# Attention steps at other units, two banks for the output sums alone, and the norm weights transposed first

## The chip, the cores and the metric

The kernel runs on one core of a Trainium2 chip. The metric is the device time of one execution in microseconds. Before the change it is 291.34 us, the median of three runs (291.09 to 291.55). The profile is of one further execution, with a span of 290.2 us from its first to its last instruction; times "at 48.06" are microseconds from the start of that span.

## The reference

Linear attention with a normalisation, and then a two-layer feed-forward network with a PReLU in between:

```python
# q, k, v: (8 batches, 8 heads, 576 positions, 64), g_norm: (64,)
kv  = np.einsum('bhsd,bhse->bhde', k, v)
o   = np.einsum('bhsd,bhde->bhse', q, kv)
rms = np.sqrt(np.mean(o * o, axis=-1, keepdims=True) + 1e-06)
x   = (o / rms * g_norm)          # to (4608 tokens, 512)
h   = x @ w_in                    # (4608, 2048)
g   = np.maximum(h, 0.0) + alpha * np.minimum(h, 0.0)
out = g @ w_out                   # (4608, 512), float32
```

## The kernel before

The 4608 tokens are handled in 9 windows of 512 (`W = 512`, w = 0 to 8). Heads go in pairs (j = 0 to 3), two heads of 64 filling the 128 rows. Window 0 is worked off by itself. From window 1 on there is one loop: in each of 16 units (`u`) of window w, TensorE makes one group of 128 hidden features of window w, some of the second product of window w - 1, and a few attention steps of window w + 1.

PSUM, where all matmuls write, is divided into pools of one 128x512 float32 bank each; a tag names one bank, or as many as `bufs` says:

```python
ps_h = ...  # tags h0, h1, h2: hidden groups (later also sums of the second product)
ps_y = ...  # tag y
ps_s = ctx.enter_context(tc.tile_pool(name="pss", bufs=1, space=bass.MemoryType.PSUM))
ps_o = ctx.enter_context(tc.tile_pool(name="pso", bufs=2, space=bass.MemoryType.PSUM))
ps_q = ctx.enter_context(tc.tile_pool(name="psq", bufs=1, space=bass.MemoryType.PSUM))
...
Q_POOL, S_POOL, O_POOL = (ps_q, "q"), (ps_s, "s"), (ps_o, "o")
```

The four attention steps of a pair. Each ends with an instruction on another engine that reads the bank; until that is done, no later tile can have the bank. `ot_ps` is held longest: by its square, and by the norm, which comes after the sum of squares.

```python
def step_t(b, j, pool=(ps_s, "s")):          # q transposed
    qt_ps = pool[0].tile([P, n_runs(b) * rows(b)], FP16, name="qt_ps", tag=pool[1])
    ...                                       # 5 transposes (6 in batch 0)
    nc.scalar.copy(out=qts[b, j][:], in_=qt_ps[:, 0:S])   # VectorE for b == 0 and j < 2

def step_kv(b, j, pool=(ps_s, "s")):
    kv_ps = pool[0].tile([P, P], FP32, name="kv_ps", tag=pool[1])
    ...                                       # 5 matmuls (6 in batch 0)
    nc.vector.tensor_mul(out=kvs[b, j][:], in0=kv_ps[:], in1=mask32[:])

def step_ot(w, j, pool=None):                 # output sums, without a pool: ps_o
    ot_ps = ps_o.tile([P, W], FP32, name="ot_ps", tag="o")
    ...                                       # one matmul for each batch in the window
    nc.scalar.activation(out=sq[:], in_=ot_ps[:], func=AF.Square)

def ssq_mm(w, j, pool=(ps_s, "s")):           # sum of squares, 1/sqrt
    nc.tensor.matmul(out=ssq_ps[:], lhsT=mask16[:], rhs=sq[:], start=True, stop=True)
    nc.scalar.activation(out=rstd[:], in_=ssq_ps[:], func=AF.Abs_reciprocal_sqrt, ...)

def norm(w, j):                               # frees ot_ps
    nc.vector.scalar_tensor_tensor(out=xts[w, j][:], in0=ot_ps[:], scalar=g2col[:],
                                   in1=rstd[:], op0=ALU.mult, op1=ALU.mult)
# step_ssq(w, j, pool) is ssq_mm and then norm
```

A hidden group (`h_ps`, `m_sb`, `gt` in the profile): four matmuls, a Relu on ScalarE into one of two `m_sb` buffers, and a VectorE instruction that frees the bank:

```python
def m1_group(w, g, pool=None):
    ...                                                   # 4 matmuls into h_ps
    nc.scalar.activation(out=m_sb[:], in_=h_ps[:], func=AF.Relu, scale=-1.0)
    nc.vector.scalar_tensor_tensor(out=gts[w, i][:, r, :], in0=m_sb[:],
        scalar=beta_sb[:, g : g + 1], in1=h_ps[:], op0=ALU.mult, op1=ALU.add)
```

The loop, cut to what concerns window 1 (all engines run their instructions in program order):

```python
Y3_AT = [(8, 8), (8, 8), (8, 8), (8, 9), (9, 9), (9, 10), (10, 10), (10, 10), (10, 11),
         (11, 11), (11, 12), (12, 12), (12, 13), (13, 14), (14, 15), (15, 16)]
for w in range(1, NW):
    ...
    for u in range(NF):                      # 16 units
        m1_group(w, G_ORDER[u])
        ...
        if w == 1 and u == 2:
            regroup(2, "k", 0, H)
        if w == 1 and u == NF - 1:
            regroup(3, "q", 0, 2)
        if w == 2 and u == 0:
            h_tags[0] = ("h1", "h2")         # from here two banks for hidden groups
        if w == 1:
            for i in range(*Y3_AT[u]):       # the last quarter of window 0's product
                y_mm(ys[3], 0, 3, i)
                if i == NF - 1:
                    y_out(ys[3], 0, 3)       # ScalarE copies the bank out
        else:
            ...                              # 7 matmuls of window w - 1
        attention(w + 1, u)
        if w == 1:
            for k in {5: (0,), 8: (1,)}.get(u, ()):
                s_sum(1, 1, k)               # two VectorE instructions on
                s_sum(1, 2, k)               #   what units 0 to 7 made
        ...
```

The front, before window 0's hidden groups (`keep_warm` is matmuls whose result nobody reads; `alpha_row` holds alpha and g_norm, loaded by three small transfers at the very start):

```python
    step_t(0, 0, h_at(0))
    keep_warm(2)
    step_kv(0, 0)
    keep_warm(1)
    step_ot(0, 0)
    regroup0("q", 1)
    keep_warm(1)
    step_t(0, 1, h_at(1))
    regroup0("k", 1)
    ssq_mm(0, 0)
    keep_warm(1)
    step_kv(0, 1, h_at(2))
    keep_warm(1)
    step_ot(0, 1)
    ...                        # alpha_ps, see the change
    step_t(0, 2, h_at(0))
    step_t(0, 3, h_at(1))
    ...                        # g2col, beta_sb and norm(0, 0), see the change
    ssq_mm(0, 1, h_at(2))
    keep_warm(2)
    regroup0("k", 2, 2)
    step_kv(0, 2, h_at(0))
    keep_warm(1)
    step_kv(0, 3, h_at(1))
    norm(0, 1)
    step_ot(0, 2, (ps_y, "y"))
    ...
```

After that come the hidden groups of window 0, and then three quarters of its second product, mixed with the attention steps of window 1, which need batch 1 of q, k and v.

Of the kernel before, what the change touches and what calls it, by code (L numbers as in the profile page):

```python
# [9 lines left out]
FP32 = mybir.dt.float32  # L10
FP16 = mybir.dt.float16
AF = mybir.ActivationFunctionType
ALU = mybir.AluOpType
# [4 lines left out]
def kernel(  # L18
# [11 lines left out]
    nc = tc.nc  # L30
# [5 lines left out]
    P = 128  # L36
# [10 lines left out]
    NF = D_FF // P  # L47
# [4 lines left out]
    const_p = ctx.enter_context(tc.tile_pool(name="constp", bufs=1))  # L52
# [10 lines left out]
    ps_y = ctx.enter_context(tc.tile_pool(name="psy", bufs=1, space=bass.MemoryType.PSUM))  # L63
# [11 lines left out]
    def early_pair(eng, nm, tag):  # L75
# [14 lines left out]
            name=nc.get_next_instruction_name(),  # L90
# [18 lines left out]
    alpha_row = ysb_p.tile([P, D_MODEL], FP32, name="y_sb")  # L109
    nc.sync.dma_start(out=alpha_row[0:NF, 0:P], in_=moe_alpha[:].rearrange("(g p) -> g p", p=P))  # L110
    for r in range(P // D):
        nc.sync.dma_start(
            out=alpha_row[NF : NF + 1, r * D : (r + 1) * D], in_=g_norm[:].unsqueeze(0)
# [7 lines left out]
    for i in range(NBUF):  # L121
        t = {}
# [39 lines left out]
    def load_batch(b, names=("k", "v", "q")):  # L162
        for nm in names:
            load_rem(b, nm)
            load_main(b, nm)

    def regroup0(nm, j, n=1):
        i, h = divmod(2 * j, HH)
        nc.vector.tensor_copy(  # L169
            out=bufs[0][nm][0:P0, :, 2 * j : 2 * (j + n), :].rearrange("p t h d -> p h t d"),  # L170
            in_=stages[0, nm, i][0:P0, h : h + 2 * n],
        )
# [40 lines left out]
    ident = const_p.tile([P, P], FP32, name="ident")  # L213
# [19 lines left out]
    def keep_warm(n, ps=warm_ps):  # L233
        for i in range(n):
            nc.tensor.matmul(out=ps[:], lhsT=warm16[:, 0:P], rhs=warm16, start=True, stop=True)
# [8 lines left out]
    def rows(b):  # L244
        return P0 if b == 0 else P

    def n_runs(b):
        return T0 if b == 0 else NT

    def pair_cols(b, nm, j):  # L250
        def f(t):
            n = rows(b)
            if nm == "v" and b == 0:
                h = 2 * j % HH
                return stages[b, nm, 2 * j // HH][0:n, h : h + 2, t, :]
            if nm == "v" and t < TPP:
                return stages[b, nm][:, 2 * j : 2 * j + 2, t, :]
            if nm == "v":
                return bufs[b % NBUF][nm][0:n, 0, 2 * j : 2 * j + 2, :]
            return bufs[b % NBUF][nm][0:n, t, 2 * j : 2 * j + 2, :]  # L260
        return f

    def step_t(b, j, pool=(ps_s, "s")):
        qs = pair_cols(b, "q", j)
        qt_ps = pool[0].tile([P, n_runs(b) * rows(b)], FP16, name="qt_ps", tag=pool[1])
        c = 0
        for t in range(n_runs(b)):
            n = rows(b)
            nc.tensor.matmul(  # L269
                out=qt_ps[:, c : c + n],  # L270
                lhsT=qs(t),
                rhs=ident16[0:n, 0:n],
                is_transpose=True,
                start=(t == 0),
                stop=(t == n_runs(b) - 1),
            )
            c += n
        qts[b, j] = attn_p.tile([P, S], FP16, name="qt_sb", tag=f"qt{j}")
        if b == 0 and j < 2:
            nc.vector.tensor_copy(out=qts[b, j][:], in_=qt_ps[:, 0:S])  # L280
        else:
            nc.scalar.copy(out=qts[b, j][:], in_=qt_ps[:, 0:S])  # L282

    def step_kv(b, j, pool=(ps_s, "s")):
        ks, vs = pair_cols(b, "k", j), pair_cols(b, "v", j)
        kv_ps = pool[0].tile([P, P], FP32, name="kv_ps", tag=pool[1])
        for t in range(n_runs(b)):
            nc.tensor.matmul(  # L288
                out=kv_ps[:],
                lhsT=ks(t),  # L290
                rhs=vs(t),
                start=(t == 0),
                stop=(t == n_runs(b) - 1),
            )
        kvs[b, j] = attn_p.tile([P, P], FP16, name="kv_sb", tag=f"kv{j}")
        nc.vector.tensor_mul(out=kvs[b, j][:], in0=kv_ps[:], in1=mask32[:])
# [26 lines left out]
    def ssq_mm(w, j, pool=(ps_s, "s")):  # L323
        ot_ps, sq = ots.pop((w, j))
        ssq_ps = pool[0].tile([P, W], FP32, name="ssq_ps", tag=pool[1])
        nc.tensor.matmul(out=ssq_ps[:], lhsT=mask16[:], rhs=sq[:], start=True, stop=True)  # L326
        rstd = attn_p.tile([P, W], FP32, name="rstd")
        nc.scalar.activation(  # L328
            out=rstd[:], in_=ssq_ps[:], func=AF.Abs_reciprocal_sqrt, bias=eps_t[:], scale=inv_d,
        )  # L330
        ots[w, j] = (ot_ps, rstd)

    def norm(w, j):
        ot_ps, rstd = ots.pop((w, j))
        xts[w, j] = xt_p.tile([P, W], FP16, name="xt", tag=f"xt{j}")
        nc.vector.scalar_tensor_tensor(  # L336
            out=xts[w, j][:], in0=ot_ps[:], scalar=g2col[:], in1=rstd[:],
            op0=ALU.mult, op1=ALU.mult,
        )
# [210 lines left out]
    Q_POOL, S_POOL, O_POOL = (ps_q, "q"), (ps_s, "s"), (ps_o, "o")  # L550

    def cast0(nm, eng_copy):
        eng_copy(
            out=bufs[0][nm][0:P0, :, 0:2, :].rearrange("p t h d -> p h t d"),
            in_=st32[nm][0:P0].rearrange("p h (t d) -> p h t d", t=T0),
        )

    def h_at(i):
        return (ps_h, f"h{i}")

    cast0("q", nc.vector.tensor_copy)
    cast0("k", nc.scalar.copy)
    step_t(0, 0, h_at(0))
    keep_warm(2)
    step_kv(0, 0)
    keep_warm(1)
# [7 lines left out]
    step_kv(0, 1, h_at(2))  # L574
    keep_warm(1)
    step_ot(0, 1)
    alpha_ps = ps_y.tile([P, NF + 1], FP32, name="alpha_ps", tag="y")
    nc.tensor.matmul(
        out=alpha_ps[:], lhsT=alpha_row[0 : NF + 1, 0:P], rhs=ident[0 : NF + 1, 0 : NF + 1],
        is_transpose=True, start=True, stop=True,  # L580
    )
    regroup0("q", 2, 2)
    keep_warm(1)
    step_t(0, 2, h_at(0))
    step_t(0, 3, h_at(1))
    g2col = const_p.tile([P, 1], FP32, name="g2col")
    nc.vector.tensor_copy(out=g2col[:], in_=alpha_ps[:, NF : NF + 1])
    beta_sb = const_p.tile([P, NF], FP32, name="beta_sb")
    nc.vector.tensor_scalar(
        out=beta_sb[:], in0=alpha_ps[:, 0:NF], scalar1=-1.0, scalar2=1.0, op0=ALU.mult, op1=ALU.add,  # L590
    )
    norm(0, 0)
    ssq_mm(0, 1, h_at(2))
    keep_warm(2)
    regroup0("k", 2, 2)
# [108 lines left out]
            ATT_AT.setdefault(3 * j + at, []).append((what, j))  # L704
    ATT_1 = {}
    for what, ats in (
        ("t", (0, 2, 4, 5)), ("kv", (4, 5, 6, 7)), ("ot", (6, 8, 10, 12)), ("ssq", (9, 10, 12, 14))
    ):
        for j, at in enumerate(ats):
            ATT_1.setdefault(at, []).append((what, j))  # L710
    ATT = {"t": step_t, "kv": step_kv, "ot": step_ot, "ssq": step_ssq}

    def attention(w, u):
        if w < NW:
            for what, j in (ATT_1 if w == 2 else ATT_AT).get(u, ()):
                if w < B or what in ("ot", "ssq"):
                    if w == 2 and what in ("kv", "ssq"):
                        pool = Q_POOL if j % 2 == 0 else O_POOL if what == "kv" else S_POOL
                        (step_kv if what == "kv" else step_ssq)(w, j, pool)
                    else:  # L720
                        ATT[what](w, j)
# [9 lines left out]
    for w in range(1, NW):  # L731
        if w + 2 < B:
            load_batch(w + 2)
        for u in range(NF):
            m1_group(w, G_ORDER[u])
            if w > 1:
                unit_sums(w, u)
# [5 lines that stand above are left out]
                h_tags[0] = ("h1", "h2")  # L743
            if w > 2 and u == 0:
                y_read(w - 2, "c12")
            if w == 1:
                for i in range(*Y3_AT[u]):
                    y_mm(ys[3], 0, 3, i)
                    if i == NF - 1:
                        y_out(ys[3], 0, 3)  # L750
            else:
                for i in range(u * PER, (u + 1) * PER):
                    prod_mm(w - 1, *Y_LIST[i])
                for what in Y_READS.get(u, ()):
                    y_read(w - 1, what)
            attention(w + 1, u)
            if w == 1:
                for k in {5: (0,), 8: (1,)}.get(u, ()):
                    s_sum(1, 1, k)
                    s_sum(1, 2, k)  # L760
            if w + 2 < B:
                for nm, j in REG_AT.get(u, ()) if w > 1 else ():
                    regroup_pair(w + 2, nm, j)
            if w == 2:
                for nm, j in REG_2.get(u, ()):
                    regroup_pair(3, nm, j)
                if u < 2:
                    s_sum(1, u + 1, 2)
# [48 lines left out]
```

## Time and profile before

| | before |
|---|---|
| time, median of 3 | 291.34 us (291.09 to 291.55) |
| span of the profile | 290.2 us |
| TensorE matmul busy | 280.6 us (97%) |
| VectorE busy | 221.2 us (76%) |
| ScalarE busy | 177.2 us (61%) |
| TensorE clock granted | 0.999 |
| first h matmul of window 0, 1, 2 | 16.14, 48.06, 69.10 us |

In the profile's lines, PE is TensorE (PEld its weight loads), DVE is VectorE, ACT is ScalarE, POOL is GpSimd, and L352 is line 352 of the kernel. A line of a timeline gives the start, the duration, the engine, the source line, what is written from what, and the idle time before it with what ended it. A line of the chain gives start, duration and what it was. Matmuls are pipelined: the duration of a row reaches beyond the start of the next one.

### The profile page before, as it was taken

To read this page: it belongs to the slowest core of one execution; us is meant where nothing else is said; L and a number is where in the kernel's file an instruction comes from. 1 tells how busy PE (TensorE), PEld (TensorE's weight loads), DVE (VectorE), ACT (ScalarE), POOL (GpSimd) and SP (SyncE) were. 2 spreads that over 40 slices of the span, in tenths; PEclk is the share of its full clock that TensorE was granted. 3 is DMA by queue.
4 is the path that set the end of the run, shared out by engine and by line. 5 is a ranking of instruction groups with operands and counts; after the bars stand their busy time and mean duration, and the time that the engine had idled before them with its cause. 6 is when DMAs were issued, how large, how long until landed. Compare 5 with 4: busy or idle time off the path is not lost.

```text
span 290.2 us, 5214 instructions
## 1 busy us (share of the span) xinstructions
PE 280.6 (97%) x1988; PEld 179.5 (62%) x1988; DVE 221.2 (76%) x420; ACT 177.2 (61%) x307; POOL 50.1 (17%) x72
## 2 busy tenths in 40 slices
PE   7899999989999999999999999999999999999994
PEld 2444544634766666667766667666666666666783
DVE  6569729878688878797778777877878788787862
ACT  2567448768878865785678668765754565443310
POOL 8743334760023210212012000000000000000001
PEclk9999999999999999999999999999999999999999
DMA  7999999999709990199019401110112011201223
GB/s 153 194 207 195 198 201 193 179 184 189 111 6 119 189 160 3 39 179 170 3 38 146 118 0 37 38 61 15 37 29 77 5 38 36 63 11 37 67 81 109
DMA packets 50397, 28.43 MB, mean 98 GB/s; under 512 B 13524, under 2 KB 50020, under 8 KB 50372
## 3 DMA queue, kind: packets, MB, share of 16 engines
q0 software_dynamic: 40064, 18.98, 50.4%
q1 hardware_dynamic: 9396, 8.24, 9.7%
q10 hardware_dynamic: 912, 0.89, 1.1%
q8 instruction: 15, 0.25, 0.3%
q14 instruction: 10, 0.08, 0.1%
HBM read 36.71 MB, written 9.44 MB: 159 GB/s over the span
## 4 chain that ended last, share of the span: by engine, by line
PE 83%; DMA 12%; DVE 1%; issue 1%; ACT 1%; POOL 1%; DVEq 0%; POOLq 0%
PE h_ps L352 38%; PE yY L501 14%; PE yZ L501 10%; PE yX L501 9%; DMA vst<-in_v_dram 5%; DMA w_in_sb<-in_moe_w_in_dram 5%; PE kv_ps L288 3%; PE ot_ps L310 3%; DMA qst<-in_q_dram 2%; PE ssq_ps L326 2%; PE qt_ps L269 2%; PE y L377 2%; DVE gt L363 1%; ACT m_sb L359 1%; DVE xt L336 0%
## 5 line engine op out<-in xcount | busy, mean ns | idle before, releaser
L352 PE MATMUL h_ps<-xt,w_in_sb 128*128 128x512 f16 x576 | 145.5, 379 | 0.5 <-DVE gt L363 0.3
L363 DVE SCALAR_TENSOR_TENSOR gt<-m_sb,beta_sb,h_ps 128x512 f16<-128x512 f32 x144 | 106.9, 745 | 45.9 <-ACT m_sb L359 44.3
L359 ACT ACTIVATE m_sb<-h_ps 128x512 f32<-128x512 f32 x144 | 86.0, 598 | 60.3 <-PE h_ps L352 46.8
L352 PEld LDWEIGHTS <-w_in_sb 128*128 128x128 f16 x576 | 54.4, 98 | 45.9 <-issue 1.4
L501 PEld LDWEIGHTS <-s 128*128 128x128 f16 x512 | 50.1, 98 | 19.3
L501 PEld LDWEIGHTS <-gt 128*128 128x128 f16 x384 | 37.6, 98 | 15.1 <-issue 0.5
L501 PE MATMUL yY<-wsum,s 128*128 128x256 f16 x256 | 36.3, 273 | 0.0
L501 PE MATMUL yX<-w_out_sb,gt 128*128 128x256 f16 x256 | 35.1, 273 | 0.0
L316 ACT ACTIVATE sq_sb<-ot_ps 128x512 f16<-128x512 f32 x36 | 21.3, 597 | 17.3 <-PE ot_ps L310 16.8
L328 ACT ACTIVATE rstd<-ssq_ps,eps_t 128x512 f32<-128x512 f32 x36 | 24.6, 688 | 9.7 <-PE ssq_ps L326 9.7
L336 DVE SCALAR_TENSOR_TENSOR xt<-ot_ps,g2col,rstd 128x512 f16<-128x512 f32 x36 | 26.5, 744 | 4.3 <-ACT rstd L328 4.3
L400 POOL DMA_DIRECT2D out_dram<-y_sb x8 | 4.4, 550 | 139.1 <-DVE y_sb L526 131.4
L282 ACT COPY qt_sb<-qt_ps 128x576 f16<-128x576 f16 x30 | 18.7, 637 | 5.8 <-PE qt_ps L269 5.7
L501 PE MATMUL yY<-wsum,gt 128*128 128x256 f16 x128 | 17.6, 273 | 0.0
L501 PE MATMUL yZ<-w_out_sb,s 128*128 128x256 f16 x128 | 17.6, 273 | 0.0
L501 PE MATMUL yZ<-wsum,s 128*128 128x256 f16 x128 | 17.6, 273 | 0.0
L377 PE MATMUL y<-w_out_sb,gt 128*128 128x512 f16 x64 | 17.1, 379 | 0.4 <-DMA w_out_sb<-in_moe_w_out_dram 0.3
L310 PE MATMUL ot_ps<-qt_sb,kv_sb 128*128 128x512 f16 (+7 forms) x64 | 13.7, 286 | 1.5 <-DVE xt L336 0.8
L143 POOL DMA_DIRECT2D vst<-in_v_dram x7 | 6.2, 888 | 48.4 <-PE kv_ps L288 44.8
L288 PEld LDWEIGHTS <-ksb 128*128 128x128 f16 (+1 forms) x164 | 11.4, 98 | 4.5 <-DVE ksb L169 1.5
L288 PE MATMUL kv_ps<-vst,ksb 128*128 128x128 f16 (+1 forms) x136 | 12.6, 219 | 1.4 <-DMA vst<-in_v_dram 0.8
L453 DVE TENSOR_TENSOR s<-s,gt 128x512 f16<-128x512 f16 x32 | 13.5, 421 | 0.5
(67 smaller groups left out, 243.0 us busy)
## 6 DMA issues: line engine op xcount, KB each, us to landing
out_dram<-y_sb SPq DMA_DIRECT2D x72, 64.0 KB, 2.2
kst<-in_k_dram POOLq DMA_DIRECT2D x7, 512.0 KB, 6.8
qst<-in_q_dram POOLq DMA_DIRECT2D x7, 512.0 KB, 10.2
vst<-in_v_dram POOLq DMA_DIRECT2D x7, 512.0 KB, 8.7
out_dram<-y_sb SPq DMA_DIRECT2D x23, 128.0 KB, 2.0
w_out_sb<-in_moe_w_out_dram POOLq DMA_DIRECT2D x4, 512.0 KB, 16.1
w_in_sb<-in_moe_w_in_dram POOLq DMA_DIRECT2D x3, 512.0 KB, 12.1
w_in_sb<-in_moe_w_in_dram POOLq DMA_DIRECT2D x2, 256.0 KB, 8.3
```

What stands on the lines that cost most here:

```text
L282: nc.scalar.copy(out=qts[b, j][:], in_=qt_ps[:, 0:S])
L288: nc.tensor.matmul(out=kv_ps[:], lhsT=ks(t), rhs=vs(t), start=(t == 0), stop=(t == n_runs(b) - 1),)
L310: nc.tensor.matmul(out=ot_ps[:, n0 - w * W : n1 - w * W], lhsT=kvs[b, j][:], rhs=qts[b, j][:, n0 - b * S : n1 - b * S], start=True, stop=True,
L316: nc.scalar.activation(out=sq[:], in_=ot_ps[:], func=AF.Square)
L328: nc.scalar.activation(out=rstd[:], in_=ssq_ps[:], func=AF.Abs_reciprocal_sqrt, bias=eps_t[:], scale=inv_d,)
L336: nc.vector.scalar_tensor_tensor(out=xts[w, j][:], in0=ot_ps[:], scalar=g2col[:], in1=rstd[:], op0=ALU.mult, op1=ALU.mult,)
L352: nc.tensor.matmul(out=h_ps[:], lhsT=w_in_blk(c, g), rhs=xts[w, c][:], start=(c == 0), stop=(c == NC - 1),)
L359: nc.scalar.activation(out=m_sb[:], in_=h_ps[:], func=AF.Relu, scale=-1.0)
L363: nc.vector.scalar_tensor_tensor(out=gts[w, i][:, r, :], in0=m_sb[:], scalar=beta_sb[:, g : g + 1], in1=h_ps[:], op0=ALU.mult, op1=ALU.add,)
L377: nc.tensor.matmul(out=y[:], lhsT=gt_cols(w, g, a * P, (a + 1) * P), rhs=w_out_blk(g), start=(g == 0), stop=(g == NF - 1),)
L453: nc.vector.tensor_sub(out=t[:], in0=sums[w, 1, k][:], in1=a11)
L501: nc.tensor.matmul(out=bank, lhsT=lhs, rhs=rhs, start=fresh, stop=(c == NK - 1), skip_group_check=True,)
```

## The change

It has two parts.

Block 1, the loop over window 1: the attention steps of window 2 move to other units. The kv steps of pairs 1 and 3, which took one of the two `ps_o` banks, take the bank of `ps_s`, so that both `ps_o` banks serve output sums alone. The outputs of pairs 0 and 1 are then made in the same unit, and the first sum of squares follows one unit after it. Two sums on VectorE move from unit 8 to unit 7. It is meant to let the output steps find a free bank.

| step of window 2 | units before, pairs 0 to 3 | units after |
|---|---|---|
| t | 0, 2, 4, 5 | 0, 2, 4, 7 |
| kv | 4, 5, 6, 7 | 4, 5, 6, 8 |
| ot | 6, 8, 10, 12 | 7, 7, 11, 12 |
| ssq and norm | 9, 10, 12, 14 | 8, 10, 12, 13 |

The front: the transpose of alpha and g_norm on TensorE, and the two VectorE instructions that read it (`g2col`, `beta_sb`), come right after the first transpose step. The norm of pair 0 comes directly behind the regroup of q for pairs 2 and 3. It is meant to take two instructions and a wait out of VectorE's way before the regroup of k.

```diff
     step_t(0, 0, h_at(0))
+    alpha_ps = ps_y.tile([P, NF + 1], FP32, name="alpha_ps", tag="y")
+    nc.tensor.matmul(
+        out=alpha_ps[:], lhsT=alpha_row[0 : NF + 1, 0:P], rhs=ident[0 : NF + 1, 0 : NF + 1],
+        is_transpose=True, start=True, stop=True,
+    )
+    g2col = const_p.tile([P, 1], FP32, name="g2col")
+    nc.vector.tensor_copy(out=g2col[:], in_=alpha_ps[:, NF : NF + 1])
+    beta_sb = const_p.tile([P, NF], FP32, name="beta_sb")
+    nc.vector.tensor_scalar(... alpha_ps[:, 0:NF] ...)
     keep_warm(2)
     step_kv(0, 0)
...
     step_ot(0, 1)
-    alpha_ps = ...             # the same matmul
     regroup0("q", 2, 2)
+    norm(0, 0)
     keep_warm(1)
     step_t(0, 2, h_at(0))
     step_t(0, 3, h_at(1))
-    g2col = ...                # the same two instructions
-    beta_sb = ...
-    norm(0, 0)
     ssq_mm(0, 1, h_at(2))
     keep_warm(2)
     regroup0("k", 2, 2)
...
     for what, ats in (
-        ("t", (0, 2, 4, 5)), ("kv", (4, 5, 6, 7)), ("ot", (6, 8, 10, 12)), ("ssq", (9, 10, 12, 14))
+        ("t", (0, 2, 4, 7)), ("kv", (4, 5, 6, 8)), ("ot", (7, 7, 11, 12)), ("ssq", (8, 10, 12, 13))
     ):
...
                     if w == 2 and what in ("kv", "ssq"):
-                        pool = Q_POOL if j % 2 == 0 else O_POOL if what == "kv" else S_POOL
+                        pool = Q_POOL if j % 2 == 0 else S_POOL
...
             if w == 1:
-                for k in {5: (0,), 8: (1,)}.get(u, ()):
+                for k in {5: (0,), 7: (1,)}.get(u, ()):
                     s_sum(1, 1, k)
                     s_sum(1, 2, k)
```

The second part uses `attention(w + 1, u)`, in which the steps of a unit stand in the order t, kv, ot, ssq.

More of the change, by code (lines that the diff above doesn't have):

```diff
@@ L563 @@
     step_t(0, 0, h_at(0))
+    alpha_ps = ps_y.tile([P, NF + 1], FP32, name="alpha_ps", tag="y")
[6 more added lines that the diff above has]
+    beta_sb = const_p.tile([P, NF], FP32, name="beta_sb")
+    nc.vector.tensor_scalar(
+        out=beta_sb[:], in0=alpha_ps[:, 0:NF], scalar1=-1.0, scalar2=1.0, op0=ALU.mult, op1=ALU.add,
+    )
     keep_warm(2)
@@ L576 @@
     step_ot(0, 1)
[L577 to L581, printed above, removed]
     regroup0("q", 2, 2)
+    norm(0, 0)
     keep_warm(1)
@@ L585 @@
     step_t(0, 3, h_at(1))
[L586 to L591, printed above, removed]
-    norm(0, 0)
     ssq_mm(0, 1, h_at(2))
```

## The prediction

> **What bounds the kernel now.** I read the page first, then the chain of waits in order of time, then the timeline of single engines around the two places that the change touches. The page's busy times and its chain of waits:
>
> ```profile
> span 290.2 us, 5214 instructions
> PE 280.6 (97%) x1988; PEld 179.5 (62%) x1988; DVE 221.2 (76%) x420; ACT 177.2 (61%) x307; POOL 50.1 (17%) x72
> PE 83%; DMA 12%; DVE 1%; issue 1%; ACT 1%; POOL 1%; DVEq 0%; POOLq 0%
> ```
>
> TensorE sets the time: 83% of the chain is its own work. What can be won lies in the other 17%. 12% is DMA, and the chain in order of time puts it at the start (rows for 1.32 to 38.80 us). VectorE and ScalarE have 1% each; read off the chain's pieces, some 3.6 us of theirs lie between 57.8 and 62.7 us, in the loop over window 1, whose attention steps for window 2 are what the diff moves (the others are near 42 and 71 us, outside of it). The chain there:
>
> ```profile
> 48.22 0.86 PE h_ps L352 x4
> 49.09 0.28 PE qt_ps L269 x5
> ...
> 52.24 0.22 PE y L377
> ...
> 53.59 0.28 PE kv_ps L288 x5
> ...
> 56.65 0.22 PE ot_ps L310 x2
> ...
> 57.77 0.61 ACT m_sb L359
> 58.38 0.02 issue
> 58.40 0.75 DVE gt L363
> 59.15 0.21 DVE kv_sb L296
> 59.36 0.04 issue
> 59.40 0.38 PE ot_ps L310 x2
> ...
> 61.31 0.75 DVE gt L363
> 62.06 0.67 DVE xt L336
> 62.73 0.05 issue
> 62.78 0.39 PE ot_ps L310 x2
> 63.17 0.21 PE ssq_ps L326
> ```
>
> The first rows give what each step costs TensorE when it flows: 0.86 us for the four matmuls of a unit, 0.28 for a transpose step, 0.28 for a kv step, 0.22 each for an ot step, a sum of squares and a y matmul. The lower rows show the chain leaving TensorE twice, each time to come back at an ot step. TensorE's timeline shows the size of the two holes:
>
> ```profile
> 58.71 0.38 PE L377 MATMUL y<-w_out_sb,gt 128*128 128x512 f16 x1
> 59.40 0.38 PE L310 MATMUL ot_ps<-qt_sb,kv_sb 128*128 128x128 f16 x2 [0.31 <-DVE kv_sb L296]
> ...
> 61.56 0.38 PE L377 MATMUL y<-w_out_sb,gt 128*128 128x512 f16 x1
> 62.78 0.39 PE L310 MATMUL ot_ps<-qt_sb,kv_sb 128*128 128x128 f16 x2 [0.84 <-DVE xt L336]
> ```
>
> A y matmul blocks the array for 0.22, so ot of pair 1 could have started at 58.93 and started at 59.40 (0.47 lost), and ot of pair 2 at 61.78 instead of 62.78 (1.00 lost). As a cross-check, the stage runs from 48.06 (first matmul of window 1) to 69.10 (first of window 2), 21.04 us; its work is 16 x 0.86 + 8 x 0.22 + 4 x (0.28 + 0.28 + 0.22 + 0.22) = 19.52, so 1.52 idle, and the two holes are 1.47 of it.
>
> For the front, the same TensorE timeline further ahead:
>
> ```profile
> 35.74 2.75 PE L377 MATMUL y<-w_out_sb,gt 128*128 128x512 f16 x12 [0.32 <-DMA w_out_sb<-in_moe_w_out_dram]
> 38.85 0.40 PE L288 MATMUL kv_ps<-vst,ksb 128*128 128x128 f16 x4 [0.36 <-DMA vst<-in_v_dram]
> ```
>
> TensorE waits twice for a transfer here: for the second quarter of w_out, then for v of batch 1. In the chain, a queue of loads (1.32 to 10.48 q, 10.76 to 24.45 w_in, 24.99 to 38.80 v) is the whole path up to 38.80.
>
> **What the Trainium skill says.** "TensorE: Matmul & The Clock Gate", Single matmul latency and Back-to-back issue gap: a warm matmul of N columns takes (398 + N)/2.4 ns alone and N/2.4 + 2.5 apart when they follow each other; for 512 that is 379 and 216. The trace agrees with both (mean 379 ns on the h_ps rows, 0.86 / 4 = 0.215 us in the chain); the lower sustained figure that the page also gives, 131 ns, is not seen here. So I count TensorE by steps of 0.216, not by its rows. "Perfetto Trace Analysis", Optimizing Scalar/DVE Operations: the profiled latency is longer than what the engine is held for, because the acknowledgement of the write overlaps the next instruction. The trace agrees: ScalarE rows of 0.60 follow each other 0.49 to 0.50 apart (60.68, 61.17), VectorE rows of 0.75 are 0.67 apart (61.31, 61.98, 62.64). I use these distances. "Perfetto Trace Analysis", Optimization Strategy: gaps that repeat on the engine that ought to be full can mean a lack of buffers. Both holes are of this kind, as follows.
>
> **The change part by part.**
>
> *The eight banks.* Output sums (ot) of window 2 use the pool of two banks; in the kernel before, kv of pairs 1 and 3 use that pool as well. The first hole: kv of pair 3 took the bank, its masked copy stands on VectorE behind gt of unit 7 (58.40 to 59.15, then 59.07 to 59.35), and ot of pair 1 needs that bank. The second hole: ot of pair 2 needs the bank of pair 0, which the norm of pair 0 frees; that norm ran at 61.98 to 62.72, since the sum of squares was asked for only in unit 9 and the norm stands behind gt of unit 9. The change sends kv of pairs 1 and 3 to the single bank of the transposes, so the ot pool holds ot alone; puts ot of pairs 0 and 1 together in unit 7; takes the first sum of squares to unit 8, the second stays in 10; and puts ot of pair 2 one unit later (11). No instruction is added or taken out. TensorE's 19.52 us stay.
>
> *New schedule by hand.* Units 0 to 4 are as before, unit 5 starts at 53.71. Adding step costs without a wait, TensorE runs: unit 5 with y and kv1 to 55.07; unit 6 with kv2 to 56.21; unit 7 with transpose 3, ot0, ot1 to 57.79; unit 8 with y, kv3, first sum of squares to 59.37; unit 9 to 60.23; unit 10 with y and second sum to 61.53; unit 11 with ot2 to 62.61; unit 12 with y, ot3, third sum to 64.13; unit 13 with y and fourth sum to 65.43; 14 and 15 with y to 67.59. Now each wait, with ScalarE and VectorE in program order at the distances above and a unit's m_sb 1.06 us after its first matmul (56.71 to 57.77):
> - kv1 takes the bank of transpose 2, whose copy is done at 54.48: no wait at 54.79.
> - kv3 takes the bank of transpose 3: m_sb of unit 7 at 57.27, then the copy 57.77 to 58.40: no wait at 58.87.
> - Then both squares (58.31, 58.86 to 59.40) hold up m_sb of unit 8 to 59.41; first rstd 59.91 to 60.6, m_sb of unit 9 at 60.50.
> - VectorE: gt of unit 7 at 57.93, the two sums of s (moved from unit 8 to 7) to 59.45, in a time when it would be idle; gt of unit 8 60.04 to 60.79, masked kv3 to 60.99, norm 0 60.92 to 61.66, gt of unit 9 61.59 to 62.34, gt of unit 10 to 63.0, norm 1 62.93 to 63.67.
> - Second sum of squares needs kv3's bank: 60.99 against 61.31, no wait. ot2 needs norm 0: 61.66 against 62.39, no wait. Unit 12 needs the bank of unit 9: 62.34 against 62.61, no wait. ot3 needs norm 1: 63.67 against 63.69, no margin at all.
>
> So the stage ends at 67.59 instead of 69.10, 1.51 earlier, if nothing slips. At its edge the last norm (69.09 to 69.84 before) came late for the fourth matmul of window 2, whose unit took 1.16 instead of 1.03; in my schedule norm 3 is done at 67.5, so that 0.13 goes as well. The next two waits (0.25 before the first yX, behind the copy of the old y, and 0.48 before unit 1, behind gt of unit 0 in the same bank) keep their causes, and at best the change is worth 1.6 us by there.
>
> I take 0.3 off for slips: ot3 has no margin, and unit 12 and the second sum have 0.3 with three instructions ahead of each. This is a choice, about one extra instruction's wait on VectorE (0.2 to 0.4 from the rows). Left: 1.3 us. After 72 us the chain is TensorE row upon row, so the rest shifts whole.
>
> *The front.* The transposed norm weights move up by about 5 us (11.28 before), to after the first transpose step (5.79). TensorE does not start kv of pair 0 until v lands (7.34), so the 0.23 us matmul is free unless the small loads land after 7.1; the alpha load was issued at 1.20 with 4.2 to landing, and the g_norm loads were issued up to 2.0, so I estimate 6.2. Taking two VectorE instructions (0.16 each) and the wait for alpha_ps (0.18) out from between the regroup of q (ends 11.36) and norm 0 lets the norm start at 11.36 instead of 11.82, regroup k at about 12.05 instead of 12.49, kv of pair 2 near 12.9 instead of 13.34, and window 0's first h matmul near 15.7 instead of 16.14: 0.44. But w_out lands at 35.7 and v at 38.8 whatever TensorE does; no wait in front of those loads names a compute engine up to 24.99. Worth 0: TensorE waits longer in the same two places.
>
> Sum: 1.3 + 0 = 1.3, and 291.34 - 1.3 = 290.0.
>
> **The rivals.**
> 1. *The single bank becomes the wait.* Transposes, kv1, kv3 and two sums of squares now share one bank, each release being an instruction in a queue of others. For it: with three ScalarE instructions in a row in unit 7, m_sb of unit 8 comes 0.56 late (59.41 for 58.85), and everything on VectorE behind it. If it slips by one more instruction at kv3 and one at ot3, 0.3 to 0.5 each, the holes are back at half size or more: 290.4 to 291.
> 2. *The front counts.* If loads or the first steps of block 1 hung on compute, 0.4 more: 289.6. Against it, the 0.32 and 0.36 of idle that name a DMA.
> 3. *The front hurts.* If the g_norm loads land late, TensorE stands still ahead of kv of pair 0. The waits at 35.7 and 38.85 swallow up to some 0.8 us of that, so I give it no loss.
> 4. *The gain is given back later,* at the first regroup of q of batch 3 (VectorE, 70.40), if that transfer were only just there. It did not wait for a DMA before, and 1.5 us earlier probably does not either.
>
> **Range and chances.** Best case 1.6 plus 0.4 of rival 2 is 289.3; rival 1 at full size is no gain, 291.3. Eight in ten: 289.4 to 290.9. Two per cent is 5.8 us, more than the 1.5 us of idle in the stage and the front's 0.44 together, so faster by over 2% is next to excluded, and slower would need new waits of four times the old ones.
>
> **What would show it.** Right: no idle ahead of ot_ps between 56 and 66 us, the span from first h matmul of window 1 to that of window 2 near 19.8 instead of 21.04, its start still near 48.06; the first h matmul of window 0 about 0.4 earlier, and more idle named DMA at 35 and 38 us. Wrong: a start of that stage other than 48.0 (the front counts), or idle ahead of kv_ps, ssq_ps or h_ps in units 8 to 13 that names VectorE or ScalarE (rival 1), or a wait for in_q_dram near 69 us (rival 4).

## The result and the profile after

| | before | changed |
|---|---|---|
| time, median | 291.21 us (291.09 to 291.55) | 290.01 us (289.61 to 290.16) |
| ratio to before, 95% interval | | 0.9955 (0.9938 to 0.9972) |
| same kernel in a second session, ratio | 291.52 us | 289.66 us, 0.9939 (0.9927 to 0.9951) |
| span of the profile | 290.2 us | 288.3 us |

The change makes the kernel 1.3 us faster by the first ratio (0.8 to 1.8), 1.8 us by the second (1.4 to 2.1). It was forecast at 1.3 us.

The page of the changed kernel, its busy times and its chain by engine:

```profile
span 288.3 us, 5215 instructions
PE 280.0 (97%) x1988; PEld 179.4 (62%) x1988; DVE 220.7 (77%) x420; ACT 176.9 (61%) x307; POOL 50.4 (17%) x72
PE 87%; DMA 7%; POOL 1%; DVE 1%; issue 1%; ACT 1%; DVEq 0%; POOLq 0%
```

The work is the same to 0.6 us on each engine; what went is waiting. The chain in order of time, over the same part of the loop over window 1 as before:

```profile
57.02 0.28 PE qt_ps L269 x5
57.30 0.44 PE ot_ps L310 x4
57.74 0.86 PE h_ps L352 x4
58.60 0.22 PE y L377
58.81 0.28 PE kv_ps L288 x5
59.09 0.22 PE ssq_ps L326
59.31 1.73 PE h_ps L352 x8
61.04 0.22 PE y L377
61.25 0.22 PE ssq_ps L326
61.47 0.86 PE h_ps L352 x4
62.33 0.22 PE ot_ps L310 x2
```

Every piece is TensorE's and starts where the last one ends. The detours over m_sb, gt, kv_sb and xt, which stood before the ot steps, are gone. The timeline of TensorE at the last two ot steps, and at the edge of window 2:

```profile
63.25 0.38 PE L377 MATMUL y<-w_out_sb,gt 128*128 128x512 f16 x1
63.47 0.38 PE L310 MATMUL ot_ps<-qt_sb,kv_sb 128*128 128x128 f16 x2
...
67.35 1.03 PE L352 MATMUL h_ps<-xt,w_in_sb 128*128 128x512 f16 x4
68.46 0.92 PE L501 MATMUL yX<-w_out_sb,gt 128*128 128x256 f16 x7
69.22 0.44 PE L269 MATMUL qt_ps<-ident,qsb 128*128 128x128 f16 x5
69.85 1.02 PE L352 MATMUL h_ps<-xt,w_in_sb 128*128 128x512 f16 x4 [0.18 <-DVE gt L363]
```

ot of pair 3 starts 0.22 after the y matmul, the distance at which matmuls flow. Two short holes are left at the edge: 67.35 to 68.46 is 1.11 for 0.86 of work, and unit 1 starts at 69.85 although the transposes end at 69.50. And TensorE's wait for the loads at the front, in the same answer as before:

```profile
35.52 2.75 PE L377 MATMUL y<-w_out_sb,gt 128*128 128x512 f16 x12 [0.19 <-DMA w_out_sb<-in_moe_w_out_dram]
38.64 0.40 PE L288 MATMUL kv_ps<-vst,ksb 128*128 128x128 f16 x4 [0.37 <-DMA vst<-in_v_dram]
```

They are still there. (`yX`, `yY` and `yZ` in the rows are sums of the second product from window 1 on.) By stages, from starts of rows in the timelines of TensorE ("v" is the first kv matmul of batch 1, "end" the start of the last 16 matmuls of yZ, which the next table uses too):

| stage | before | changed |
|---|---|---|
| first h matmul of window 0, at | 16.14 | 16.05 |
| v, at | 38.85 | 38.64 |
| v to first h matmul of window 1 | 9.21 | 9.20 |
| window 1 to window 2 | 21.04 | 19.51 |
| window 2 to first yX | 1.11 | 1.11 |
| yX to unit 1 of window 2 | 1.52 | 1.39 |
| unit 1 to end | 212.43 | 212.42 |
| v to end | 245.31 | 243.63 |

So from v on the change is worth 1.68 us: 1.53 in the stage of window 1 and 0.13 at its edge (the rest is rounding). The other 0.21 of the 1.89 between the profiles is the landing of v.

### The profile page after: what moved, and what is told of

Its sections match the earlier page's. It is cut to its first block, busy times and chain, and to the rows that moved or that the text cites. A ratio compares the mean times of both kernels' runs of the same rounds, so it can differ in the third digit from the quotient of the medians.

```text
span 288.3 us, 5215 instructions
## 1 busy us (share of the span) xinstructions
PE 280.0 (97%) x1988; PEld 179.4 (62%) x1988; DVE 220.7 (77%) x420; ACT 176.9 (61%) x307; POOL 50.4 (17%) x72
## 3 DMA queue, kind: packets, MB, share of 16 engines
q1 hardware_dynamic: 9396, 8.24, 9.7%
## 4 chain that ended last, share of the span: by engine, by line
PE 87%; DMA 7%; POOL 1%; DVE 1%; issue 1%; ACT 1%; DVEq 0%; POOLq 0%
PE h_ps L352 41%; PE yY L501 15%; PE yZ L501 10%; PE yX L501 9%; DMA vst<-in_v_dram 7%; PE kv_ps L288 3%; PE ot_ps L310 3%; PE ssq_ps L326 2%; PE y L377 2%; PE qt_ps L269 2%; POOL kst L135 1%; DVE xt L336 1%; ACT rstd L328 0%; POOL vst L135 0%; POOL qst L135 0%
## 5 line engine op out<-in xcount | busy, mean ns | idle before, releaser
L296 DVE TENSOR_TENSOR kv_sb<-kv_ps,mask 128x128 f16<-128x128 f32 x32 | 9.1, 285 | 6.4 <-PE kv_ps L288 6.4
```

## The experiments

Theory: the gain is the two holes of block 1, and the front gives nothing since loads hold TensorE later. Rivals: the front carries part of it; the bank alone or the units alone would do; and for the margins, that VectorE's queue has room. The times below are each against the kernel before on the same chip. From v on TensorE's rows repeat to some 0.02 us in the same kernel, so v to end tells small effects apart that the times can't. There is one exception: in turn and y3_early a later load, v of batch 2, adds 0.06 and 0.18 us that are not the edit's (see y3_early).

| kernel | median us | ratio to before, 95% | v at | v to end |
|---|---|---|---|---|
| block_only | 289.73 | 0.9936 (0.9921 to 0.9950) | 37.77 | 243.64 |
| front_only | 291.28 | 0.9994 (0.9985 to 1.0002) | 37.95 | 245.29 |
| front_late2 | 290.13 | 0.9947 (0.9929 to 0.9965) | 38.68 | 243.64 |
| front_late8 | 290.41 | 0.9962 (0.9950 to 0.9975) | 39.08 | 243.55 |
| ot2_at_11 | 290.35 | 0.9967 (0.9954 to 0.9980) | 38.36 | 244.26 |
| banks_only | 292.23 | 1.0019 (1.0008 to 1.0030) | 39.23 | 245.91 |
| sums_at_8 | 290.13 | 0.9958 (0.9946 to 0.9970) | 37.97 | 244.34 |
| turn | 289.79 | 0.9944 (0.9927 to 0.9961) | 38.70 | 243.51 |
| changed | 289.66 | 0.9939 (0.9927 to 0.9951) | 38.15 | 243.63 |
| y3_early | 289.93 | 0.9948 (0.9935 to 0.9962) | 38.25 | 243.81 |
| turn_sums | 289.45 | 0.9932 (0.9918 to 0.9946) | 38.28 | 243.31 |
| best | 289.13 | 0.9922 (0.9910 to 0.9934) | 38.16 | 243.27 |

### The two parts alone

**block_only**: the kernel before with these lines of the change and nothing else.

```diff
-        ("t", (0, 2, 4, 5)), ("kv", (4, 5, 6, 7)), ("ot", (6, 8, 10, 12)), ("ssq", (9, 10, 12, 14))
+        ("t", (0, 2, 4, 7)), ("kv", (4, 5, 6, 8)), ("ot", (7, 7, 11, 12)), ("ssq", (8, 10, 12, 13))
-                        pool = Q_POOL if j % 2 == 0 else O_POOL if what == "kv" else S_POOL
+                        pool = Q_POOL if j % 2 == 0 else S_POOL
-                for k in {5: (0,), 8: (1,)}.get(u, ()):
+                for k in {5: (0,), 7: (1,)}.get(u, ()):
```

> The kernel before with the second part of the change alone: steps, banks and the two sums of block 1; the front as before. My theory (the front is worth nothing, since two transfers hold TensorE at 35.5 and 38.6 us): 1.2 us faster than before, as the whole change, and the stage from the first h matmul of window 1 to that of window 2 takes 19.5 us as in the changed kernel. Rival (the front carries a part of it): a gain smaller by 0.1 to 0.4 us.

Its ratio is that of the whole change (0.9936 and 0.9939), its stage of window 1 takes 19.51 us, and v to end is 243.64. The whole gain is in this part.

**front_only**: the rest of the change alone.

```diff
     step_t(0, 0, h_at(0))
+    alpha_ps, g2col, beta_sb = ...       # moved here
...
     regroup0("q", 2, 2)
+    norm(0, 0)                           # moved here
```

> The kernel before with the first part of the change alone: alpha and g_norm transposed first, norm of pair 0 behind the regroup of q. My theory: no change (within 0.2 us of before), first h matmul of window 0 about 0.1 us earlier as in the changed kernel, and the v of batch 1 still ends TensorE's wait near 38.6 to 38.9. Rival: 0.1 to 0.4 us faster.

v to end is 245.29 against 245.31 before, and the time is 0.9994, an interval that holds 1: at most 0.4 us, and 0 is not excluded. On VectorE the order works as meant:

```profile
10.86 0.72 DVE L169 COPY qsb<-qst 96x1536 f16<-96x1536 f16 x1
11.50 0.73 DVE L336 SCALAR_TENSOR_TENSOR xt<-ot_ps,g2col,rstd 128x512 f16<-128x512 f32 x1
12.16 0.54 DVE L169 COPY ksb<-kst 96x1536 f16<-96x1536 f16 x1
```

The regroup of k starts at 12.16 where it started at 12.49. But the first h matmul of window 0, at 15.60 here, is at 15.19 in block_only, which has the old front. It lay between 15.19 and 16.38 over the four profiles with the old front and between 15.49 and 16.05 over eight with the new one. The ranges overlap because the very first kv step already starts anywhere from 6.58 to 7.82 us. Counted from that step, window 0's first h matmul comes after 8.54 to 8.80 us with the old front and after 8.24 to 8.62 with the new one; the means are 8.63 and 8.38. So the new order gains some 0.25 us ahead of window 0, and they end in the wait for v: here TensorE is done with the y matmuls before it at 37.56 and starts kv at 37.95.

**front_late2** and **front_late8**: the changed kernel, with useless matmuls added on TensorE in the front.

```diff
-    keep_warm(1, warm_late)
+    keep_warm(3, warm_late)      # front_late8: keep_warm(9, warm_late)
     step_ot(0, 3, Q_POOL)
```

> The changed kernel with two more warming matmuls ahead of ot of pair 3 in window 0: 2 x 0.216 = 0.43 us more on TensorE in the front. In the changed kernel TensorE idles 0.35 before w_out's second quarter (transposes end at 35.17, next y at 35.52) and 0.53 before v of batch 1 (38.11 to 38.64), 0.88 in all. My theory: no change against the changed kernel, 290.0. Rival (the front is on the path): 290.4.

> The changed kernel with eight more warming matmuls at that place, 1.73 us on TensorE, of which about 0.1 fills idle time there. My theory: the two waits swallow 0.88, so 0.7 to 0.9 us slower than the changed kernel, 290.8, and no wait for w_out or v is left. Rival (the front is on the path): 1.6 to 1.7 slower, 291.7. Rival (more slack than I see): no change.

With two more, the times don't decide: the ratio of 0.9947 lies between the two of the changed kernel (0.9955 and 0.9939), the median is 0.4 us above block_only in the same session, and the interval excludes neither no change nor 0.4 more. The timeline of TensorE does decide:

```profile
35.56 2.75 PE L377 MATMUL y<-w_out_sb,gt 128*128 128x512 f16 x12 [0.43 <-DMA w_out_sb<-in_moe_w_out_dram]
38.68 0.40 PE L288 MATMUL kv_ps<-vst,ksb 128*128 128x128 f16 x4 [0.36 <-DMA vst<-in_v_dram]
```

TensorE still stands still for both loads, 0.60 us before w_out (the transposes end at 34.96) and 0.53 before v, so the added work doesn't reach the end. With eight more, window 0's first h matmul comes at 17.39, 1.34 after the changed kernel's 16.05, and both waits are gone, as the timeline of TensorE in front_late8 shows:

```profile
35.37 1.28 PE L269 MATMUL qt_ps<-ident,qsb 128*128 128x128 f16 x20
36.49 2.75 PE L377 MATMUL y<-w_out_sb,gt 128*128 128x512 f16 x12
39.08 0.39 PE L288 MATMUL kv_ps<-vst,ksb 128*128 128x128 f16 x4
```

Each row starts where the work before it ends. Against the changed kernel's first profile, 0.44 of the 1.34 us arrive at kv (39.08 against 38.64); the waits swallowed 0.90, and I had read 0.88 of idle. Against its second profile 0.93 of 1.51 arrive (kv at 38.15, h at 15.88), because the idle time before v is only 0.32 there (12 y matmuls from 35.24) and there is none before w_out. The times agree no better: the loss is 0.2 and 0.7 by the two ratios of the changed kernel, and by the medians of the same session 0.7 against block_only and 0.3 against front_late2. The rival of 1.6 to 1.7 is excluded, the exact slack is not settled.

One more rival is settled by the traces: that v itself comes later when TensorE is late. In all fourteen profiles v of batch 1 lands 13.8 us after GpSimd issued it, and the issue lies between 23.91 and 25.37 us. In front_late8, where TensorE is 1.3 us late, it is at 24.31, earlier than the changed kernel's 24.77. So the front is off the path, by 0.88 us in the changed kernel's first profile and at least 0.32 in its second, and an earlier start can't reach the end while v is what TensorE waits for.

### The two holes, one at a time

**ot2_at_11**: the kernel before with one number changed.

```diff
-    ("ot", (6, 8, 10, 12))
+    ("ot", (6, 8, 11, 12))
```

> The kernel before with a single number changed: ot of pair 2 in unit 11 instead of 10, so that unit 11's matmuls stand between the y matmul (ending 61.78) and it. Theory of the two holes: norm of pair 0 ends at 62.72, ot of pair 2 would start near 62.7, so the second hole of 1.00 us goes to under 0.1 and the first (0.47) stays: 1.0 us faster than before, 290.2. Rival (the wait only moves, to ot of pair 3 or to a hidden bank): under 0.5 us faster.

v to end falls by 1.05 (245.31 to 244.26), the time to 0.9967 of before (1.0 us less). Its timeline of TensorE:

```profile
58.25 0.38 PE L377 MATMUL y<-w_out_sb,gt 128*128 128x512 f16 x1
58.94 0.38 PE L310 MATMUL ot_ps<-qt_sb,kv_sb 128*128 128x128 f16 x2 [0.31 <-DVE kv_sb L296]
...
61.52 1.03 PE L352 MATMUL h_ps<-xt,w_in_sb 128*128 128x512 f16 x4
62.39 0.38 PE L310 MATMUL ot_ps<-qt_sb,kv_sb 128*128 128x128 f16 x2
```

The first hole stands as before (58.47 to 58.94), the second is filled by the four matmuls of unit 11, and nothing after it pays. Nearly two thirds of the whole gain are this one number.

**banks_only**: the kernel before with kv of pairs 1 and 3 in the bank of the transposes, at the old units.

```diff
-                        pool = Q_POOL if j % 2 == 0 else O_POOL if what == "kv" else S_POOL
+                        pool = Q_POOL if j % 2 == 0 else S_POOL
```

> The kernel before with only the bank of kv of pairs 1 and 3 changed (the bank of the transposes), all units as before. Theory: units and banks belong together; the first hole (0.47) goes, but in unit 5 kv of pair 1 now stands right behind the transpose of pair 3 in the same bank and must wait for its copy (ends at 55.91 where kv could begin at 55.07), a new hole of about 0.85; so 0.2 to 0.6 us slower than before. Rival (the bank alone is the cause): 0.4 to 0.5 us faster.

```profile
55.20 0.44 PE L269 MATMUL qt_ps<-ident,qsb 128*128 128x128 f16 x5
56.37 0.38 PE L288 MATMUL kv_ps<-vst,ksb 128*128 128x128 f16 x4 [0.73 <-ACT qt_sb L282]
...
60.01 0.38 PE L377 MATMUL y<-w_out_sb,gt 128*128 128x512 f16 x1
60.22 0.38 PE L310 MATMUL ot_ps<-qt_sb,kv_sb 128*128 128x128 f16 x2
...
62.38 0.38 PE L377 MATMUL y<-w_out_sb,gt 128*128 128x512 f16 x1
63.76 0.39 PE L310 MATMUL ot_ps<-qt_sb,kv_sb 128*128 128x128 f16 x2 [0.99 <-DVE xt L336]
```

In the timeline of TensorE the first hole is gone (60.01 to 60.22), and its place is taken by one of 0.89 in unit 5: the transposes end at 55.48, kv of pair 1 waits for the copy of the transposed q and starts at 56.37. The second grew from 1.00 to 1.16. Together +0.60 from v to end and 1.0019 in time: slower. Freeing the bank pays only when the transpose of pair 3 leaves unit 5. The reverse, the new units with the old banks, wasn't tried: kv of pair 3 would ask for a bank that only norm 0 frees, and that norm's sum of squares stands behind this kv in TensorE's order, so by the program each would wait for the other. No run shows it.

### VectorE's margin

**sums_at_8**: the changed kernel with the two sums back in unit 8.

```diff
-                for k in {5: (0,), 7: (1,)}.get(u, ()):
+                for k in {5: (0,), 8: (1,)}.get(u, ()):
```

> The changed kernel with the two sums of unit 7 back in unit 8, where they stand on VectorE between norm 0 and gt of unit 9. Theory (VectorE's queue has little margin behind unit 8): gt of unit 9 ends at 62.8 instead of 61.9, unit 12 waits for its bank by 0.4 and ot of pair 3 for norm 1 by 0.2 more: 0.6 us slower than the changed kernel, 290.6. Rival (there is margin; the sums' move does nothing): no change.

```profile
61.53 0.38 PE L310 MATMUL ot_ps<-qt_sb,kv_sb 128*128 128x128 f16 x2
62.17 1.02 PE L352 MATMUL h_ps<-xt,w_in_sb 128*128 128x512 f16 x4 [0.26 <-DVE gt L363]
63.03 0.38 PE L377 MATMUL y<-w_out_sb,gt 128*128 128x512 f16 x1
63.49 0.39 PE L310 MATMUL ot_ps<-qt_sb,kv_sb 128*128 128x128 f16 x2
```

TensorE's timeline has the two holes that were expected: 61.75 to 62.17 (0.42, bank of unit 9) and 63.25 to 63.49 (0.24, norm 1). The stage takes 20.18, +0.67. So the move of two instructions of 0.42 us on an engine that is 77% busy is worth two fifths of the gain. The medians are 0.1 and 0.5 us above the two of the changed kernel, which by themselves would not settle it.

### What is left at the edge

**turn**: unit 1 of window 2 takes the other of the two hidden banks.

```diff
             if w == 2 and u == 0:
                 h_tags[0] = ("h1", "h2")
+                h_turn[0] = 1
```

> The changed kernel with the turn of the hidden banks set so that unit 1 of window 2 takes bank h1, not h2 which unit 0 has just filled. In the changed kernel the transposes end at 69.50 and unit 1 starts at 69.85, waiting for gt of unit 0. Theory: the wait of 0.35 goes and stays gone, 289.65. Rival (it comes back at unit 2 or later because two banks are too few): under 0.1.

yX to unit 1 falls from 1.39 to 1.04, as expected, but only 0.12 of the 0.35 is left at the end: unit 1 to end grows by 0.16, and the stage of window 1 was 0.06 longer in this run (the load of v of batch 2, see y3_early). So the turn itself is worth about 0.19. In the timeline of the weight loads the 0.16 has a name:

```profile
72.52 0.43 PEld L501 LDWEIGHTS <-s 128*128 128x128 f16 x4
73.19 0.10 PEld L501 LDWEIGHTS <-s 128*128 128x128 f16 x1 [0.25 <-DVE s L453]
```

The fifth weight load of product 6, one of seven parts of the second product, waits for the second sum of k = 2 on VectorE.

**turn_sums**: that sum moved to unit 0 in addition.

```diff
-                if u < 2:
-                    s_sum(1, u + 1, 2)
+                if u == 0:
+                    s_sum(1, 1, 2)
+                    s_sum(1, 2, 2)
```

> The kernel with the other turn of the hidden banks, and in addition the second sum of k = 2 in unit 0 of window 2 instead of unit 1. With the turn alone, unit 1 started 0.35 earlier, but 0.15 came back in unit 2, where product 6 waited for a sum on VectorE. Theory: that sum is the second of k = 2, so the 0.15 goes as well: 0.35 less than the changed kernel from kv of batch 1 to the end, 243.3. Rival (the sums of k = 3 or gt are what is late): 243.4 to 243.5 as with the turn alone.

243.31, and unit 1 to end is 212.43 again: the second wait was that sum. By the medians 0.2 us below the changed kernel, which their intervals don't separate.

**changed**: the changed kernel again, beside these three.

> The changed kernel as it is, once more, on one chip with the next three. All theories: 289.9 to 290.1, and whatever the landing of v of batch 1 is in this run, 243.63 us from the first kv matmul of batch 1 to the start of the last 16 matmuls, of which 19.51 in the stage of window 1.

Met to the hundredth from v on; the time was a little lower than expected (289.66).

**y3_early**: the last y matmul of window 0 one unit earlier.

```diff
-(12, 13), (13, 14), (14, 15), (15, 16)]
+(12, 13), (13, 14), (14, 16), (16, 16)]
```

> The changed kernel with the last y matmul of window 0 in unit 14 instead of 15, so that ScalarE copies its bank before m_sb of unit 15 and not behind it. In the changed kernel the first matmuls of window 2 take 1.11 us to the first yX, where four matmuls take 0.86: 0.25 of waiting for that bank. Theory: 0.86 to 0.9, and 0.2 to 0.25 us faster than the changed kernel from kv of batch 1 to the end. Rival (the saved time is lost again at unit 1, which waits for gt of unit 0 in its bank): nothing, and the stretch from yX to unit 1 grows from 1.39 to 1.6.

The theory missed, and the rival holds: the move gives nothing. v to end is 0.18 longer than in the changed kernel, but not through the move, as TensorE's timeline shows:

```profile
52.54 0.44 PE L269 MATMUL qt_ps<-ident,qsb 128*128 128x128 f16 x5
53.01 0.38 PE L288 MATMUL kv_ps<-vst,ksb 128*128 128x128 f16 x4
...
66.28 1.89 PE L352 MATMUL h_ps<-xt,w_in_sb 128*128 128x512 f16 x8
68.00 0.93 PE L501 MATMUL yX<-w_out_sb,gt 128*128 128x256 f16 x7
...
69.64 1.02 PE L352 MATMUL h_ps<-xt,w_in_sb 128*128 128x512 f16 x4 [0.20 <-DVE gt L363]
```

The 0.18 is lost in unit 4, ten units ahead of the moved y matmul: the transposes end at 52.82 and kv of pair 0 starts at 53.01, where it follows them without a gap in the changed kernel. The timeline names no cause, but a late load fits. v of batch 2, which this step reads, was issued at 38.73 and landed 14.2 us later, at 52.9; in the changed kernel it took 13.8 and was there 0.3 us ahead. turn shows the same with a landing after 14.1 us and a gap of 0.07; the other profiles have no gap there.

At the edge, the hole before yX closes (the eight matmuls from 66.28 end at 68.00, and yX starts there) and comes back before unit 1: yX to unit 1 is 1.64; the rival had said 1.6. Unit 1 waits for gt of unit 0, which starts 21.39 us after the stage does (68.84) against 21.21 in the changed kernel (69.05). The difference is the 0.18 of unit 4 again. The matmuls of unit 0, from which this gt is made, start 19.69 us after the stage does (four matmuls behind 66.28) against 19.51, so they too run no earlier when a y matmul and those of unit 15 change places. The hole before yX was not on the path.

**best**: all of these, and ot of pair 2 of block 0 one y matmul later.

```diff
-    y_run(0, (8, 9, 10))
-    step_ot(1, 2)
-    y_run(0, (11,))
+    y_run(0, (8, 9, 10, 11))
+    step_ot(1, 2)
```

> The changed kernel with all of these: the y matmul in unit 14, the turn, the sum, and in the steps of block 0 the ot of pair 2 one y matmul later (it waited 0.2 us for the norm of pair 0 before). Theory: each closes its own hole, 0.25 + 0.35 + 0.2 = 0.8 less from kv of batch 1 to the end, 242.8, and 289.2 in all. Rival (the holes are one queue of VectorE's, so that closing one opens the next): 0.3 to 0.4 less.

243.27, 0.36 less than the changed kernel: turn_sums does 0.32 of it, so the rival holds. v to window 1 is still 9.20, since the hole ahead of ot of pair 2 moved to ot of pair 3, which waits for norm 1. It is the fastest of all here, 289.13 us, 0.9922 of before.

## Why the prediction was right, and where its sizes were off

- *Two holes, both from the ot pool's banks.* Right. Both are gone together. ot2_at_11 takes away the second alone and gains 1.05, where 1.00 was read; in banks_only the bank alone takes away the first, though a new hole costs more.
- *The stage shrinks from 21.04 to 19.5.* The hand schedule gave 1.51, the stage gave 1.53. The order of the margins was right too: ot of pair 3 came closest, norm 1 ending at 63.27 with ot at 63.47.
- *0.3 taken off for slips.* This is the term that was mis-sized: it measured 0. The 1.3 of the sum came out as 1.68 from v on. That the median of 290.01 nevertheless met the forecast of 290.0 is luck: v lands at another time in each run, and the same kernel was 1.3 us faster than before in one session and 1.8 in the other. Norm 1 ended 0.18 earlier, counted from the start of the stage, than in the schedule, so even the step without margin had some. The margin is real, though: sums_at_8 spends it and loses 0.67.
- *0.13 at the edge.* Right. The first group of window 2 is down from 1.16 to 1.03; yX starts after 1.11 as before, since it waits for the copy of the old y, and the 0.13 shows at unit 1. Unit 1 waits for gt of unit 0, which now starts 1.70 us after that group instead of 1.83.
- *The front is worth 0.* Not told apart from 0 (front_only), and off the path by front_late2 and front_late8. The 0.44 by which window 0 was to start earlier measured 0.09 in the changed kernel's profile: VectorE was free for the regroup of k at 12.15, which then waited 0.20 for its load, and kv of pairs 2 and 3 waited for v (0.19 on TensorE, 0.28 on its weight loads). Over all profiles, counted from the first kv step, it is about 0.25. The sign "more idle named DMA" didn't come: the idle time ahead of the two loads was 1.01 before and is 0.88, as v landed 0.21 earlier.
- *The start of the stage as a sign.* Any start other than 48.0 was to mean that the front counts. This sign was no good: the stage starts at 47.84 here, and at 46.98 in block_only, which has the old front. It follows the landing of v.
- *The norm weights land in time.* Right: the transpose ran at 6.02 without a wait, before v came at 7.43.
- *Rivals.* The single bank did not become the wait at the new units; at the old units it does (banks_only). q of batch 3 was there in time: its regroup ran at 68.63 without waiting for a load.

## What to carry to other kernels

When an engine at 97% stands still for a microsecond, ask which buffer the next step needs, which instruction frees it and what stands before that in the other engine's order; then put a block of independent work between the two, which here was one number. A buffer's pool and the order of steps have to be changed together: the same bank at the old units cost 0.6 us. And before closing a further hole, follow what starts after it: at the edge of window 2 the visible hole before yX was not on the path, and closing it gained nothing.

## What the runs showed of the hardware

From the first kv matmul of batch 1 on, the same program repeats to about 0.02 us over 200 us (243.63, 243.63 and 243.64 in the changed kernel twice and block_only), as long as v of batch 2 is there in time. What scatters is the loads ahead of it: in the twelve profiles in which TensorE had not been delayed on purpose, that matmul came at 37.77 to 39.23 us. The transfer it waits for took 13.8 us in every profile; what moved was its issue, behind the loads before it. This scatter of 1.46 us is nearly as much as the whole change is worth, so the effect of single steps was read from v on and not from the totals. Even there one late load, v of batch 2 with 14.2 instead of 13.8 us to landing, came with a loss of 0.18 us. Before a difference of this size is put down to an edit, the two timelines have to be compared row by row up to the first place where they part.
